# First layer of batch 0 with split operands instead of two plain blocks, in a fused attention and two-MLP kernel

## The chip, the cores and the metric

One core of a Trainium2 chip. The metric is the device time of one launch in microseconds (us), median of several runs.

## The reference

Attention over 4 batches, 12 heads, 448 positions and 64 channels per head, followed by two feed-forward networks on all 4 x 448 = 1792 tokens (width 768):

```
q_n, k_n = rmsnorm(q, g_q), rmsnorm(k, g_k)
attn = softmax(q_n @ k_n.T / 8);  x = (attn @ v) as 1792 x 768
h = sigmoid(x @ w_gate) * (x @ w_val);  y = h @ w_out        # 768 -> 1536 -> 768
r = relu(y @ w_in2) ** 2;               out = r @ w_out2     # 768 -> 2048 -> 768
```

The weights come as 64-bit floats and are converted on the core. The results must keep float32 accuracy.

## The kernel before

**Order of the work.** A prologue computes the attention of batch 0, two heads (a pair) at a time, six pairs. A first sweep (`sweep(0)`) then runs both networks of batch 0 with the attention of batch 1 in its gaps, a second sweep those of batch 1 with the attention of batches 2 and 3, and a last part does both networks of batches 2 and 3 together.

**Weights.** A block is 128 x 768 weights. Each goes through four steps that `next_block` keeps a few blocks ahead of their use (`w_ahead`): `w_load` (the 64-bit block into one of three `raw64` buffers, on SP's queue), `w_conv` (L167 on ACT, L171 and L175 on DVE make float32 of it in one of three `wraw` buffers), `w_store` (the float32 block to memory for the later sweeps, by a DMA that POOL issues), and `w_split` (L193 on ACT casts it to a high part in the multiplier's faster format fp32r, L194 on DVE leaves the low part, both in one of four `wsp` buffers).

**Products.** The activations are split the same way: `x_hi` (L365, ACT) and `x_lo` (L371, DVE) for each pair of heads. `mm3` then makes a product of three fp32r matmuls, high by high, high by low, low by high (all through `mm`, L566). The first two blocks of the first sweep are made otherwise: with `NPLAIN = 2` they are converted straight into a part of the tile `area`, not split, and multiplied in plain float32 (L915, 6 matmuls a block, each two records in the trace) by the unsplit attention output `xplain`. Behind each of these two blocks three `x_hi` and three `x_lo` follow, which the later blocks need.

**The prologue's order.** It is a list written by hand: `at(key, step)`, sorted by key, four keys to a pair of heads (`t = 4 * hp + c` for chunk c of pair hp). For a chunk, `s_mm` makes scores (L291, PE), `s_max` their maxima (L297, DVE), `s_exp` the exponentials (L309, ACT), `c_mm` transposes them (L327, PE), `c_copy` copies the transposes out (L336 on ACT, L337 on DVE). For a pair, `pv_mm` multiplies by v (L345) and transposes the reciprocal sums (L350), then come `x_rec` (L356, ACT) and `x_sum` (L361, DVE). The next pairs' inputs are squared, scaled (`stat_hat`, L265, DVE, after a power on POOL, L261), transposed (`a_mm`, L571, PE) and copied (`a_copy`, L283 on DVE, L285 on ACT). Into this list come loads, conversions and splits of the first weight blocks. Matmul accumulators are four tiles `acc`; a tile is reused when it has been copied out. A scheduler in the framework turns the list into a fixed order for each engine, and each engine runs its own in order; the first sweep is also its to arrange, while PE's order from the second sweep on is the program's.

Of the kernel before, what the change touches and what calls it, by code (L numbers as in the profile page):

```python
# [17 lines left out]
def attention_moe_moe2_kernel(  # L18
# [19 lines left out]
    KD = DM // 128  # L38
# [33 lines left out]
    def acc_tile():  # L72
        return acc_p.tile([128, 512], F32, tag="acc", name="acc")

    def att_tile():
        return att_p.tile([128, 2, 512], F32, tag="att", name="att")
# [21 lines left out]
    NB = len(one_sweep)  # L98
    W4 = NB - K2
    K4 = K2 // 2  # L100
    NPLAIN = 2
    wt = [[dram_p.tile([128, 768], F32, tag=f"wt{t}{g}", name=f"wt{t}{g}") for g in range(K4 // 2)] for t in range(4)]
    w32 = [dram_p.tile([128, 768], F32, tag=f"w{i}", name=f"w{i}") for i in range(NB)]
    w1s = [dram_p.tile([128, 1536], F32, tag=f"ws{p}", name=f"ws{p}") for p in range(K1)]
# [49 lines left out]
    def w_conv():  # L154
# [5 lines left out]
        lo, hi = r[:, :, 0], r[:, :, 1]  # L160
        if i < NPLAIN:
            t = plain_w[0][:, 768 * i:768 * (i + 1)]
# [21 lines left out]
    def w_split():  # L184
        i = pos["split"]
        pos["split"] += 1
        if pos["store"] <= i < NB:
            w_store()
        t = wraw.pop(i)
        if i < NPLAIN:  # L190
            return
        sp = wsp_p.tile([128, 2, 768], F32R, tag="wsp", name="wsp")
        nc.scalar.copy(out=sp[:, 0], in_=t)  # L193
        nc.vector.tensor_tensor(out=sp[:, 1], in0=t, in1=sp[:, 0].bitcast(F32), op=ALU.subtract)  # L194
        wsp[i] = sp

    def w_ahead(i):
        while True:
            if pos["split"] <= min(i + 3, pos["conv"] - 1):
                w_split()  # L200
            elif pos["conv"] <= min(i + (3 if pos["conv"] < NPLAIN + 2 else 4), pos["load"] - 1, pos["split"] + 2):
                w_conv()
# [155 lines left out]
    def x_sum(st):  # L358
        r = st["r"]
        dst = xplain[0][:, st["hp"]] if st["b"] == 0 else r  # L360
        nc.vector.tensor_tensor(out=dst, in0=st["o"], in1=r, op=ALU.mult)  # L361
        st["o"] = dst

    def x_hi(st):
        hi = nc.scalar.copy(out=xtile[st["b"]][:, 0, st["hp"]], in_=st["o"])  # L365
        if st["b"] == 0:
            tc.keep_in_program_order(hi)

    def x_lo(st):
        x, hp = xtile[st["b"]], st["hp"]  # L370
        nc.vector.tensor_tensor(out=x[:, 1, hp], in0=st.pop("o"), in1=x[:, 0, hp].bitcast(F32), op=ALU.subtract)  # L371
# [154 lines left out]
    xtile, xplain, xwhole = {}, {}, {}  # L526
# [16 lines left out]
    def block():  # L543
        wb = next_block()
        flush()
        return wb

    def flush():
        for fn, args in mid:
            fn(*args)  # L550
        mid.clear()

    def half(s, kk):
        return s == 1 and kk in (1, 3)
# [20 lines left out]
    def mm3(o, wb, kk, xh, xl, start, stop):  # L575
        wh, wl = wb[:, 0, kk], wb[:, 1, kk]
        mm(out=o, lhsT=wh, rhs=xh, start=start, stop=False)
        mm(out=o, lhsT=wh, rhs=xl, start=False, stop=False)
        mm(out=o, lhsT=wl, rhs=xh, start=False, stop=stop)

    def tmp(name):
        return tmp_p.tile([128, 512], F32, tag="tmp", name=name)[:, :N]
# [318 lines left out]
    def sweep(s):  # L901
# [5 lines left out]
        for m in range(K1):  # L907
            for i in range(2):
                o = acc_tile()[:, :N]
                wb = block()  # L910
                for kk in range(KD):
                    if s == 0 and m == 0 and i == 0 and kk == KD - 1:
                        yield
                    if s == 0 and 2 * m + i < NPLAIN:
                        nc.tensor.matmul(  # L915
                            out=o, lhsT=wb[:, 0, kk], rhs=xplain[0][:, kk],
                            start=(kk == 0), stop=(kk == KD - 1))
                    else:
                        mm3(o, wb, kk, x[:, 0, kk], x[:, 1, kk], kk == 0, kk == KD - 1)
                    if half(s, kk):  # L920
                        yield
                        flush()
                if s == 0 and 2 * m + i < NPLAIN:
                    for hp in range(3 * (2 * m + i), min(KD, 3 * (2 * m + i) + 3)):
                        st = {"b": 0, "hp": hp, "o": xplain[0][:, hp]}
                        x_hi(st)
                        x_lo(st)
                if i == 0:
                    t = tmp("t")
                    e = tmp("e")  # L930
                    nc.scalar.activation(out=e, in_=o, func=AF.Relu, scale=-1.0)
                    nc.scalar.activation(out=t, in_=o, func=AF.Abs)
                    nc.scalar.activation(out=e, in_=e, func=AF.Exp, scale=-1.0)
                    nc.scalar.activation(out=t, in_=t, func=AF.Tanh, scale=0.5)
                else:
                    nc.vector.tensor_tensor(out=e, in0=o, in1=e, op=ALU.mult)
                    nc.vector.scalar_tensor_tensor(out=e, in0=t, scalar=1.0, in1=e, op0=ALU.add, op1=ALU.mult)
                    nc.scalar.copy(out=ht[:, 0, m], in_=e)
                    low.tensor_tensor(out=ht[:, 1, m], in0=e, in1=ht[:, 0, m].bitcast(F32), op=ALU.subtract)
                yield  # L940
        y = xbuf(s)
        for j2 in range(KD // 2):
            for i in range(2):
                o = acc_tile()[:, :N]
# [21 lines left out]
        for m2 in range(K2 // 2):  # L966
            for i in range(2):
                m = 2 * m2 + i
                o = acc_tile()[:, :N]
# [6 lines left out]
                t = tmp("rl")  # L976
# [20 lines left out]
        for hf in range(2):  # L997
            accs = [acc_tile() for _ in range(nt)]
            for kb in range(K2 // 2):
                wb = block()  # L1000
                for c, (rr, c0, row) in enumerate(chunks):
                    o = accs[c][:, :384]
# [17 lines left out]
    pairs = {}  # L1020
# [152 lines left out]
    def prologue():  # L1173
# [22 lines left out]
        def at(key, fn, *args):  # L1196
            plan.append((key, len(plan), fn, args, rush[0]))
# [9 lines left out]
        def acc4():  # L1207
            return acc_tile().rearrange("p (k c) -> p k c", k=NF + 1)

        for i in range(len(keys)):  # L1210
            t = 4 * i
# [26 lines left out]
        for hp in range(HP):  # L1238
            key = (0, hp)
            rush[0] = (30, 300, 0)[min(hp, 2)]  # L1240
            for c in range(QC):
                t = 4 * hp + c
                at(t, lambda key=key, c=c: s_mm(pairs[key], c, att_tile()))
                at(t, lambda key=key, c=c: s_max(pairs[key], c))
                at(t + 0.5, lambda key=key, c=c: s_exp(pairs[key], c))
                at(t + 1.75, lambda key=key, c=c: c_mm(pairs[key], c, acc4(), acc4()))
                at(t + 2.25, lambda key=key, c=c: c_copy(pairs[key], c, (act, dve)))
            at(t + 2.5, lambda key=key: s_rec(pairs[key]))
            at(t + 3, lambda key=key: pv_mm(pairs[key], acc_tile()[:, :S], acc_tile()[:, :S]))
            at(t + 3.75, lambda key=key: x_rec(pairs[key]))  # L1250
            at(t + 4.25, lambda key=key: x_sum(pairs[key]))
        rush[0] = 0
        for t in (6, 9, 12, 15, 18, 20, 22, 24, 25):
            at(t, w_load)
        for c, t in ((0, 14), (1, 15), (0, 18), (1, 19), (0, 20), (1, 20.6), (0, 22), (1, 22.6), (0, 24), (1, 24.6), (0, 26), (1, 26.6)):
            at(t, w_split if c else w_conv)
        plan.sort(key=lambda e: e[:2])
        n = 0
# [107 lines left out]
```

## Time and profile before

| what | us |
|---|---|
| median of 3 runs | 1252.28 (1250.48 to 1255.31) |
| the profiled execution | 1250.23 |
| its span, first to last instruction | 1248.5 |
| PE busy | 1229.1 (98%) |
| DVE busy | 949.5 (76%) |
| ACT busy | 791.8 (63%) |
| mean granted TensorE clock | 0.997 of full speed |

The span is 1.7 us short of the execution's time. PE is the matmul engine, PEld its weight loads, DVE the vector engine, ACT the scalar engine, POOL GpSimd, and SP the queue that starts most transfers. A busy share is that of the time in which an instruction of the engine was under way; matmuls overlap, so the spacing of their starts says more than their durations. The order of the stages in time: prologue up to about 94 us, first sweep to about 403 us.

### The profile page before, as it was taken

How to read it: one execution, taken by the hardware profiler on the slowest of the kernel's cores; microseconds unless marked ns; L12 is line 12 of the kernel's file. 1: busy time of each engine (PE TensorE's matmuls, PEld its weight loads, DVE VectorE, ACT ScalarE, POOL GpSimd, SP SyncE). 2: the span in 40 equal slices, each digit the busy share in tenths (PEclk: the TensorE clock that was granted, in tenths of full speed). 3: DMA queues.
4: the chain of work that ended last, by engine and by line, in shares of the span. 5: the costliest groups of instructions: out<-in, count | busy, mean ns of one | idle time of the engine just before them, and what ended most of it. 6: DMA issues, size and time to landing. Idle time of an engine off the chain costs nothing.

```text
span 1248.5 us, 19159 instructions
## 1 busy us (share of the span) xinstructions
PE 1229.1 (98%) x6611; PEld 1081.9 (87%) x6611; DVE 949.5 (76%) x1494; ACT 791.8 (63%) x1605; POOL 224.8 (18%) x236
## 2 busy tenths in 40 slices
PE   8999999999999999999999999999999999999998
PEld 6547878878889988999898899999999999999998
DVE  6877988778975878888888766878875326879872
ACT  5776888667765877876798755675664223335451
POOL 3312222211120122232222110011222001110000
PEclk9999999999999999999999999999999999999999
DMA  5555999888896666787777443467798435775443
GB/s 129 122 173 197 297 319 282 264 260 245 257 311 187 153 152 162 174 188 183 172 186 174 116 112 87 136 176 179 198 225 204 98 98 145 174 179 143 127 141 112
DMA packets 200545, 225.81 MB, mean 181 GB/s; under 512 B 83968, under 2 KB 178176, under 8 KB 200448
## 3 DMA queue, kind: packets, MB, share of 16 engines
q1 hardware_dynamic: 177024, 175.36, 48.8%
q0 software_dynamic: 21568, 48.77, 17.9%
q8 instruction: 52, 0.85, 0.3%
q10 hardware_dynamic: 1856, 0.46, 0.2%
q14 instruction: 45, 0.37, 0.1%
HBM read 185.99 MB, written 76.28 MB: 210 GB/s over the span
## 4 chain that ended last, share of the span: by engine, by line
PE 86%; ACT 4%; DVE 3%; DMA 3%; issue 2%; SPq 1%; ACTq 0%; DVEq 0%
PE acc L566 55%; PE att L566 18%; PE att L571 3%; PE att L291 3%; DMA raw<-in_moe_w_gate_dram 2%; PE acc L345 2%; PE att L345 2%; PE acc L571 1%; PE acc L327 1%; PE att L327 1%; DMA wraw<-w 1%; ACT wraw L167 1%; DVE wsp L194 1%; ACT p L309 1%; ACT wsp L193 0%
## 5 line engine op out<-in xcount | busy, mean ns | idle before, releaser
L566 PE MATMUL acc<-xy,wsp 128*128 128x448 f32 x1404 | 310.8, 372 | 1.1 <-ACT rl L978 0.6
L193 ACT CAST wsp<-wraw 128x768 fp32r<-128x768 f32 x248 | 207.3, 837 | 161.0 <-PE acc L566 74.5
L194 DVE TENSOR_TENSOR wsp<-wraw,wsp 128x768 fp32r<-128x768 f32 x248 | 237.3, 958 | 84.6 <-ACT wsp L193 82.3
L566 PEld LDWEIGHTS acc<-xy,wsp 128*128 128x128 f32 x1404 | 258.5, 188 | 30.5 <-issue 6.4
L566 PE MATMUL att<-parts,wsp 128*128 128x448 f32 x720 | 152.4, 365 | 0.0
L566 PEld LDWEIGHTS att<-parts,wsp 128*128 128x128 f32 x720 | 135.1, 188 | 10.8
L566 PE MATMUL acc<-parts,wsp 128*128 128x448 f32 x540 | 116.0, 365 | 0.0
L261 POOL TENSOR_TENSOR ms<-ms,mhalf 112x16 f32<-112x16 f32 (+1 forms) x25 | 76.8, 3073 | 189.5 <-DVE ms L260 189.5
L566 PE MATMUL acc<-wsp,rb 128*128 128x384 f32 x576 | 109.6, 340 | 0.0
L566 PEld LDWEIGHTS acc<-parts,wsp 128*128 128x128 f32 x540 | 101.3, 188 | 8.0
L566 PEld LDWEIGHTS acc<-wsp,rb 128*128 128x128 f32 x576 | 100.4, 189 | 2.4 <-issue 2.0
L566 PE MATMUL acc<-hb,wsp 128*128 128x448 f32 x432 | 95.2, 371 | 0.0
L566 PE MATMUL acc<-h,wsp 128*128 128x448 f32 x432 | 87.7, 365 | 0.0
L566 PEld LDWEIGHTS acc<-hb,wsp 128*128 128x128 f32 x432 | 79.3, 188 | 9.3 <-issue 2.7
L566 PEld LDWEIGHTS acc<-h,wsp 128*128 128x128 f32 x432 | 81.1, 188 | 6.4
L167 ACT ACTIVATE wraw<-raw 128x768 f32<-128x768 f32 x66 | 60.2, 916 | 32.3 <-DVE wsp L194 16.6
L182 POOL DMA_DIRECT2D w<-wraw x66 | 36.5, 553 | 220.4 <-DVE wraw L175 202.0
L458 ACT ACTIVATE p<-att,nm 112x448 f32<-112x448 f32 x96 | 60.1, 631 | 17.2 <-DVE nm L447 16.2
L309 ACT ACTIVATE p<-att,nm 112x448 f32<-112x448 f32 x88 | 55.3, 637 | 17.9 <-DVE nm L297 16.3
L566 PE MATMUL acc<-wsp,rp 128*128 128x384 f32 x360 | 64.0, 334 | 0.0
L175 DVE SCALAR_TENSOR_TENSOR wraw<-wraw,raw 128x768 int32<-128x768 int32 x66 | 62.9, 954 | 0.9
L566 PEld LDWEIGHTS acc<-wsp,rp 128*128 128x128 f32 x360 | 62.6, 188 | 0.0
(205 smaller groups left out, 1992.3 us busy)
## 6 DMA issues: line engine op xcount, KB each, us to landing
wraw<-w SPq DMA_DIRECT2D x80, 384.0 KB, 3.6
w<-wraw POOLq DMA_DIRECT2D x66, 384.0 KB, 6.3
raw<-in_moe_w_out_dram SPq DMA_DIRECT2D x28, 768.0 KB, 6.6
wraw<-w SPq DMA_DIRECT2D x92, 192.0 KB, 2.6
raw<-in_moe_w_in_dram SPq DMA_DIRECT2D x16, 768.0 KB, 6.0
raw<-in_moe_w_gate_dram SPq DMA_DIRECT2D x12, 768.0 KB, 6.7
raw<-in_moe_w_val_dram SPq DMA_DIRECT2D x12, 768.0 KB, 7.1
ws<-w POOLq DMA_DIRECT2D x48, 192.0 KB, 4.8
```

Source lines behind the costliest of these rows:

```text
L167: size = nc.scalar.activation(out=t, in_=hi.bitcast(F32), func=AF.Prelu, scale=2.0 ** -112, alpha=2.0 ** 32)
L175: nc.vector.scalar_tensor_tensor(out=ti, in0=ti, scalar=3, in1=hi, op0=ALU.logical_shift_left, op1=ALU.bitwise_or)
L182: nc.gpsimd.dma_start(out=w32[i], in_=wraw[i])
L193: nc.scalar.copy(out=sp[:, 0], in_=t)
L194: nc.vector.tensor_tensor(out=sp[:, 1], in0=t, in1=sp[:, 0].bitcast(F32), op=ALU.subtract)
L261: nc.gpsimd.tensor_tensor(out=ms, in0=ms, in1=mhalf[:QR, 0:ms.shape[1]], op=ALU.pow)
L291: nc.tensor.matmul(out=ps[:QR, e, :S], lhsT=kq[a, 1, c * QR:(c + 1) * QR], rhs=kq[a, 0], start=True, stop=True)
L309: nc.scalar.activation(out=p[:, e], in_=ps[:QR, e, :S], func=AF.Exp, bias=nm[:, e:e + 1], scale=st["rq"][:, c, e:e + 1] if "rq" in st else ...
L345: nc.tensor.matmul(out=o[e * D:(e + 1) * D], lhsT=v[:, kc, e], rhs=pt[:, (NF + 1) * e + kc if kc < NF else NF], start=(kc == 0), stop=(kc ...
L458: nc.scalar.activation(out=p[:, i * S:(i + 1) * S], in_=ps[:QR, i, :S], func=AF.Exp, bias=nm[:, i:i + 1], accum_out=su[:, c, e:e + 1])
L566: m = latest[0] = nc.tensor.matmul(**kw)
L571: m = nc.tensor.transpose(*a)
```

## The change

No block is plain any more (`NPLAIN = 0`), so the first two blocks are converted into `wraw` buffers, split, and multiplied by `mm3` like the others. The `x_hi` and `x_lo` of each pair of heads stand in the prologue's list behind its `x_sum`. The list has six conversions and six splits of weights as before, with some keys changed; before, the first two splits did nothing but start the store. The nine `w_load` entries stand in the list before and after.

```diff
-    NPLAIN = 2
+    NPLAIN = 0
...
-                if s == 0 and 2 * m + i < NPLAIN:
-                    for hp in range(3 * (2 * m + i), min(KD, 3 * (2 * m + i) + 3)):
-                        st = {"b": 0, "hp": hp, "o": xplain[0][:, hp]}
-                        x_hi(st)
-                        x_lo(st)
...
             at(t + 4.25, lambda key=key: x_sum(pairs[key]))
+            at(t + 4.4, lambda key=key: x_hi(pairs[key]))
+            at(t + 4.45, lambda key=key: x_lo(pairs[key]))
...
-        for c, t in ((0, 14), (1, 15), (0, 18), (1, 19), (0, 20), (1, 20.6), (0, 22), (1, 22.6), (0, 24), (1, 24.6), (0, 26), (1, 26.6)):
+        for c, t in ((0, 14), (1, 15), (0, 18), (1, 19), (0, 19), (1, 20), (0, 22), (1, 23), (0, 24), (1, 24.6), (0, 25.5), (1, 26)):
             at(t, w_split if c else w_conv)
```

DVE's order where the first block is converted, in the attention of the third and fourth pair (`raw` is the 64-bit block, `nm` the maxima, `xy_267` the split activations):

```order
 L171 TENSOR_SCALAR raw_555<-raw_555 128x768
 L260 TENSOR_SCALAR ms<-ms 112x16
-L175 SCALAR_TENSOR_TENSOR area<-area,raw_555 128x768
+L175 SCALAR_TENSOR_TENSOR wraw<-wraw,raw_555 128x768
+L194 TENSOR_TENSOR wsp<-wraw,wsp 128x768
 L361 TENSOR_TENSOR xplain<-acc,rs 128x448
 L297 TENSOR_REDUCE nm<-att 112x2
 L337 COPY area<-acc 128x3x112
-L297 TENSOR_REDUCE nm<-att 112x2
-L316 TENSOR_SCALAR su<-su 112x8
+L371 TENSOR_TENSOR xy_267<-xplain,xy_267 128x448
+L297 TENSOR_REDUCE nm<-att 112x2
```

The low part of the block (L194) now stands ahead of `x_sum` and of the chunk maxima, and the low part of the activations (L371) ahead of the next maxima.

PE's order from the last pair's score matmuls to the first sweep, before:

```order
L915 MATMUL acc<-xplain,area 128x448 x4
L327 MATMUL acc<-ident,p 128x112 x3
L915 MATMUL acc<-xplain,area 128x448
L327 MATMUL acc<-ident,p 128x112 x11
L345 MATMUL acc<-area,v_93 64x448
L350 MATMUL acc<-ident,sb 128x112 x4
L345 MATMUL acc<-area,v_93 64x448 x7
L915 MATMUL acc<-xplain,area 128x448 x5
L566 MATMUL acc<-xy_267,wsp 128x448 x9
L915 MATMUL acc<-xplain,area 128x448 x2
L566 MATMUL acc<-xy_267,wsp 128x448 x56
```

and with the change:

```order
L566 MATMUL acc<-xy_267,wsp 128x448 x12
L327 MATMUL acc<-ident,p 128x112 x5
L566 MATMUL acc<-xy_267,wsp 128x448
L327 MATMUL acc<-ident,p 128x112 x2
L566 MATMUL acc<-xy_267,wsp 128x448 x2
L327 MATMUL acc<-ident,p 128x112 x7
L345 MATMUL acc<-area,v_93 64x448
L350 MATMUL acc<-ident,sb 128x112 x4
L345 MATMUL acc<-area,v_93 64x448 x7
L566 MATMUL acc<-xy_267,wsp 128x448 x101
```

Ahead of the last pair's `pv_mm` (L345) stood 5 of the 12 plain matmuls and now stand 15 of the 36 that replace them. Further on, the first sweep's attention instructions stand at other places among the matmuls, up to some blocks apart; from the start of the second sweep every engine's order is the same again.

ACT's order ahead of the last pair's `pv_mm`, with the change:

```order
L309 ACTIVATE p,su<-att,nm 112x448 x2
L167 ACTIVATE wraw<-raw_955 128x768
L167 ACTIVATE wraw<-raw_1019 128x768
L336 COPY area<-acc 128x4x112 x2
L167 ACTIVATE wraw<-raw_1082 128x768
L356 COPY rs<-acc 128x448
L365 CAST xy_267<-xplain 128x448
L193 CAST wsp<-wraw 128x768
```

Before, the same two conversions stood between the last exponentials and the two copies, and one split (L193) and two more `x_hi` behind them. The last L193 shown is now that of the fifth block, which waits until PE has used up the first block's `wsp` buffer.

## Rows read from the trace of the kernel before

**Rows 1.** The page's busy times, and its chain of work by engine:

```profile
PE 1229.1 (98%) x6611; PEld 1081.9 (87%) x6611; DVE 949.5 (76%) x1494; ACT 791.8 (63%) x1605; POOL 224.8 (18%) x236
...
PE 86%; ACT 4%; DVE 3%; DMA 3%; issue 2%; SPq 1%; ACTq 0%; DVEq 0%
```

**Rows 2.** PE's waits over the span: us in total, times, longest us.

```profile
PE acc L327 <- ACT p L309: 2.3, 4, 0.8
PE acc L571 <- DVE qk L265: 1.8, 1, 1.8
...
PE att L327 <- ACT p L309: 1.3, 2, 0.8
...
PE acc L566 <- DVE wsp L194: 1.1, 2, 0.7
...
PE acc L327 <- DVE area L337: 0.8, 1, 0.8
```

**Rows 3.** Timeline of PE, prologue: start us, us, line, tiles, count [idle before].

```profile
53.60 3.23 PE L345 MATMUL acc<-pt,v 128*64 128x448 f32 x16
...
65.32 3.23 PE L345 MATMUL acc<-area,v 128*64 128x448 f32 x16
...
76.46 3.23 PE L345 MATMUL acc<-pt,v 128*64 128x448 f32 x16
...
89.01 0.96 PE L345 MATMUL acc<-area,v 128*64 128x448 f32 x2
...
93.59 4.03 PE L915 MATMUL acc<-xplain,area 128*128 128x448 f32 x10
```

**Rows 4.** Timeline of PE, first sweep.

```profile
100.43 11.85 PE L566 MATMUL acc<-xy,wsp 128*128 128x448 f32 x56
...
119.35 3.52 PE L566 MATMUL acc<-xy,wsp 128*128 128x448 f32 x16 [0.38 <-DVE wsp L194]
```

**Rows 5.** Busy by engine (PE, PEld, DVE, ACT, POOL), granted clock, DMA share, GB/s.

```profile
40.00:60.00 20.00, 20.00 (x121) 9.68 (x120) 17.16 (x30) 15.69 (x40) 7.54 (x5) 1.00 0.18 38
60.00:80.00 20.00, 19.04 (x117) 9.71 (x117) 16.00 (x27) 16.21 (x41) 3.10 (x6) 1.00 0.55 165
80.00:100.00 20.00, 19.23 (x84) 10.27 (x81) 14.76 (x23) 11.03 (x22) 2.79 (x5) 1.00 0.78 246
```

**Rows 6.** Groups by line and shape, 0 to 200 us: count, busy us, mean ns.

```profile
L194 DVE TENSOR_TENSOR wsp<-wraw,wsp 128x768 fp32r<-128x768 f32 x25 | 23.7, 951 | 3.6 <-ACT wsp L193 3.3
...
L193 ACT CAST wsp<-wraw 128x768 fp32r<-128x768 f32 x25 | 21.0, 846 | 0.6 <-DVE wraw L175 0.6
...
L915 PE MATMUL acc<-xplain,area 128*128 128x448 f32 x24 | 9.9, 548 | 0.0
...
L371 DVE TENSOR_TENSOR xy<-xplain,xy 128x448 fp32r<-128x448 f32 x6 | 3.5, 619 | 0.0
```

**Rows 7.** Timeline of DVE: first conversion, and keys of the sixth pair.

```profile
56.30 0.96 DVE L175 SCALAR_TENSOR_TENSOR area<-area,raw 128x768 int32<-128x768 int32 x1
...
64.30 0.61 DVE L283 COPY kq<-acc 128x448 f32<-128x448 f32 x1
```

**Rows 8.** Timeline of ACT, end of the prologue.

```profile
86.37 1.72 ACT L167 ACTIVATE wraw<-raw 128x768 f32<-128x768 f32 x2
88.00 0.93 ACT L336 COPY area<-acc 128x448 f32<-128x448 f32 x2
...
92.12 1.50 ACT L365 CAST xy<-xplain 128x448 fp32r<-128x448 f32 x3
```

**Rows 9.** Busy by engine and granted clock, around PE's longest wait for `stat_hat`.

```profile
450.00:460.00 10.00, 8.21 (x38) 7.16 (x37) 7.57 (x14) 7.02 (x17) 2.53 (x4) 0.83 0.96 195
460.00:470.00 10.00, 10.00 (x58) 9.18 (x57) 8.53 (x14) 8.48 (x20) 2.27 (x3) 1.00 0.91 193
```

**Rows 10.** Timelines of POOL and DVE, a power and a split at the same time.

```profile
447.08 2.93 POOL L261 TENSOR_TENSOR ms<-ms,mhalf 112x16 f32<-112x16 f32 x1 [13.59 <-DVE ms L260]
...
448.15 0.95 DVE L194 TENSOR_TENSOR wsp<-wraw,wsp 128x768 fp32r<-128x768 f32 x1
```

## The prediction

> **What bounds the kernel now.** I read the page first. PE is busy for 98% of the span, and the chain that ended last runs through PE for 86% of it [rows 1]. So the time is PE's work and PE's waits, and an edit counts only where it alters one of the two. PE's waits over the whole span come next: they are few, mostly under 1 us, and the ones that this change can touch are those of the transposes for exponentials (L327), of a transpose for a DVE copy, and of a matmul for a weight split [rows 2]. The third view is PE's timeline over the prologue: two pairs of heads begin their products with v 11.72 us apart (53.60 and 65.32), the next 11.14 (76.46), the last 12.55 (89.01), with ten records of plain matmuls in between [rows 3]. The fourth says what else is loaded there: from 40 to 80 us DVE is busy for 80 to 86% and ACT for 78 to 81%, while between 80 and 100 ACT falls to 55% [rows 5]. The reader is to see that the prologue is PE's too, but with DVE close behind it. From 100 us on PE's order is one long row of matmuls with one short wait at 119 [rows 4].
>
> **The change part by part.** Times below are against the profiled execution, 1250.23 us (span 1248.5 and 1.7 around it); it is 2.05 below the median of the runs shown, 1252.28.
>
> *Matmul work.* Twelve plain matmuls go, 24 records. Ten of them last 4.03 us, of which the last one's own length is 0.55 [rows 3, 6], so they follow each other by (4.03 - 0.55) / 9 = 0.387, and 24 take 9.3 us. They become 36 fp32r matmuls, which follow each other by 11.85 / 56 = 0.21 [rows 4], 7.6 us. PE gets back 1.7 us, all of it on the path. Bounds: with 0.35 (3.48 over all ten) and 0.40 (4.03 over ten) for a record it is 0.8 and 2.0.
>
> *The pairs of heads.* What PE saves is paid for on DVE and ACT, ahead of the last pair's product with v. DVE gets two more splits there (L194, 0.95 us) and five `x_lo` (L371, 0.62), 5.0 us together; ACT two more casts (L193, 0.85) and five `x_hi` (L365, 0.5), 4.2 us [rows 6, 8]. The sixth `x_lo` and two further splits lie behind that product, under matmuls, and cost nothing while three blocks (54 matmuls, 11 us) are ready. Nor does the store of the first blocks cost: it leaves from `wraw` in place of `area`, and the next conversion into that buffer comes some 20 us later. The nine loads are nine before and after, and move no queue that PE waits for. In DVE's order the added L194 and L371 stand ahead of chunk maxima; behind these wait ACT's exponentials, and behind those PE's transposes. I went through the changed order by hand from 53 us on, with the spacings of the trace. The first block's conversion ends at 57.2 as before [rows 7]. Its cast and low part follow, so the next maxima are 0.9 us later and, behind the `x_lo`, those after them 1.3. DVE's copy of the sixth pair's keys, which frees the accumulator of the fourth pair's product with v, starts at 65.6 in place of 64.30 [rows 7], so that product starts at 66.3 (before 65.32). The fifth pair's then starts at 78.1 (before 76.46), as the second and third block are both split in front of it. The last pair's starts at 89.3 (before 89.01 [rows 3]): there ACT is what PE waits for, with two conversions and two copies behind the last exponentials, in the order they had before [rows 8]. Two `x_lo` of the earlier pairs may cost another 0.1 each, so 89.5. By then PE has made 15 matmuls of the first layer in place of ten records, 3.15 against 3.9 us, so with no new wait it would have been there at 88.3. The pairs thus cost 1.2 us of new waits. Bounds: 1.5 gained, if the waits before these transposes (0.8 on DVE's copy, 0.7 of the 2.3 on exponentials [rows 2]) vanish and no new one comes; 5.0 lost, if all that DVE gets falls on PE. I take 1.2, nearer the first, since DVE has 2.3 us spare in each 11.7 [rows 5].
>
> *The weights behind.* Block 7's split was late by 0.38 us at 119 [rows 4]. Now the first `wsp` buffer comes free at about 99.7, when the first block's last matmul is through, and the conversions behind it on ACT and DVE run some 5 us earlier than before; I expect the split about 2.7 us ahead of its use. That is 0.4 back. Bounds: 0 and 0.4.
>
> *The rest of the first sweep.* Its attention instructions stand at other places, with the same work. Two of the waits on exponentials, 1.3 us in all, lie here [rows 2], and may go or come again. I take 0, with 1.3 gained as one end and a wait like the 1.8 us one before `stat_hat` as the other [rows 2]. That one cost more than itself: around it PE began 38 matmuls in 10 us, where the next 10 us hold 58, so it took 20 / 58 of 10 us, 3.4 us, 1.6 of them because the granted clock was 0.83 on the mean, that is a third of the time at 1.2 GHz and not 2.4 [rows 9]. From the second sweep on nothing is moved.
>
> Sum: -1.7 + 1.2 - 0.4 = **-0.9 us**, 1249.3 for a profiled execution and 1251.4 for the median.
>
> **A rule against it.** A split that ran inside a power on POOL took 0.95 us, its mean, and the power 2.93, so neither held up the other [rows 6, 10]. The Trainium skill (SBUF — State Buffer, Who interferes with whom) says that a DVE instruction with two SBUF inputs and a GpSimd instruction that reads SBUF lock each other out, the one that issues second for all of the other's time. By that rule the added split would wait for the whole power; the trace does not agree.
>
> **The rivals.**
> - *DVE becomes the bound of the pairs.* The added 5.0 us fall on PE in full, and waits of more than a microsecond bring the lower clock as at 452 us, 1.6 more [rows 9]: -2.1 + 5.0 + 1.6 = +4.5, 1256.8. With `x_hi` (2.5 us) in series it would be 1259.3. For it: DVE's 86% [rows 5], and that maxima stand behind the added work. Against: DVE's spare time. It decides once the last product with v starts after 90.4 (88.3 and the 2.1 saved): from there the kernel is slower than before. Chance 0.20.
> - *All waits go.* -1.7 - 0.4 - 1.5 - 1.3 = -4.9, 1247.4. For it: the new order has more blocks ready early, and matmuls of the first layer fill PE between transposes. Against: the same exponentials must still come. Chance 0.15.
> - *The first sweep's new order makes one long wait*, as at 452: -0.9 + 3.4 = +2.5, 1254.8. For it: several hundred instructions change places, and DVE is then at over 80%. Against: there the trace has 0.38 and two waits under 1 us. Chance 0.15.
> - *DVE held off by POOL.* The added split of the first block falls into the power that POOL starts beside the conversion, and DVE stands still for up to that power's 2.93 us: -0.9 + 2.9 = +2.0, 1254.3. Chance 0.03, as the row speaks against it [rows 10].
>
> **How the numbers follow.** The forecast has the 0.47 that is left. About 0.5% of the time, 6.3 us, is what a measurement of this kernel can tell from no change. None of the gains adds up to that: 4.9 is all there is, so faster has 0.04, for the scatter of the medians. Slower needs DVE's work in series with ACT's: 0.08. The same has 0.88. The range goes from all waits gone, 1247.4, to DVE's work in full, 1256.8, with the outermost tenths left out: 1247.2 to 1256.4.
>
> **What would show it.** Right: L915 is gone, the last product with v starts between 88.5 and 90.4, the wait of block 7 is gone, and the first layer's matmuls follow each other by 0.21 from there on. The profile of the changed kernel would show DVE at 85% or more between 60 and 90 us. Wrong: that product starts after 90.4, or PE's waits between 100 and 400 us add up to more than 3 us, or the granted clock falls there. If block 7 still waits, the reasoning on the buffers is wrong, too.

## The result, and the profile after

The kernel after takes 1257.35 us (median of 9 runs, from 1254.57 up), the one before 1250.48 (9 runs, 1247.27 to 1256.22). One run of the kernel after, 6749.57 us, was disturbed, and the comparison leaves it out (the median of the other eight is 1256.67). The ratio is **1.0054**, with a 95% interval of 1.0039 to 1.0068: the change makes the kernel slower by 0.54%, 6.8 us (4.9 to 8.5 by the interval). The profiled execution took 1258.77 us. From its page, the span, the busy times and the chain, as in [rows 1]:

```profile
span 1257.0 us, 19177 instructions
...
PE 1233.2 (98%) x6623; PEld 1083.8 (86%) x6623; DVE 951.2 (76%) x1496; ACT 794.7 (63%) x1607; POOL 226.1 (18%) x236
...
PE 83%; DVE 5%; ACT 5%; DMA 3%; issue 2%; SPq 2%; POOL 0%; DVEq 0%; ACTq 0%; POOLq 0%
```

PE, DVE and ACT do nearly the work that they did. What has grown is the part of the chain that runs through DVE and ACT, from 7% to 10%: PE waits more for them. These shares only say where to look: three points are 38 us of the span, many times the loss. PE's timeline over the pairs of heads, to set beside [rows 3]:

```profile
56.00 3.23 PE L345 MATMUL acc<-pt,v 128*64 128x448 f32 x16
...
64.15 1.22 PE L327 MATMUL acc<-ident,p 112*128 112x112 f32 x7 [0.86 <-ACT p L309]
...
69.03 3.23 PE L345 MATMUL acc<-area,v 128*64 128x448 f32 x16
...
77.01 1.01 PE L291 MATMUL att<-kq 64*112 64x448 f32 x4 [0.85 <-ACT p L309]
...
79.29 1.22 PE L327 MATMUL acc<-ident,p 112*128 112x112 f32 x7 [0.44 <-ACT p L309]
...
81.37 0.97 PE L345 MATMUL acc<-pt,v 128*64 128x448 f32 x2
...
93.53 0.96 PE L345 MATMUL acc<-area,v 128*64 128x448 f32 x2 [1.10 <-ACT area L336]
...
98.10 20.74 PE L566 MATMUL acc<-xy,wsp 128*128 128x448 f32 x101
```

From the third product with v to the last it is 93.53 - 56.00 = 37.53 us, where it was 89.01 - 53.60 = 35.41. That is 2.1 us more, behind three waits on exponentials and one on a copy by ACT, 3.25 us together; before there were two, of 0.74 and 0.77. The first layer then runs 101 matmuls without a wait, and block 7's of [rows 4] is gone. The same stretches as in [rows 5], busy by engine and granted clock:

```profile
60.00:80.00 20.00, 17.55 (x109) 9.03 (x106) 18.03 (x30) 17.05 (x41) 5.71 (x6) 1.00 0.54 159
80.00:100.00 20.00, 18.89 (x97) 10.70 (x98) 15.19 (x25) 12.14 (x26) 2.77 (x5) 1.00 0.59 181
```

From 60 to 80 us, where this execution runs 2.4 us behind the one before, DVE went from 80% to 90% and ACT from 81% to 85%, and PE from 95% to 88%.

The second loss stands where the first sweep ends. PE's timeline there, of the kernel before:

```profile
373.15 2.55 PE L566 MATMUL acc<-wsp,rb 128*128 128x384 f32 x13
375.54 0.84 PE L327 MATMUL att<-ident,p 112*128 112x112 f32 x7
376.14 1.30 PE L566 MATMUL acc<-wsp,rb 128*128 128x384 f32 x6
377.28 0.93 PE L571 MATMUL att<-ident,qk 112*128 112x112 f32 x8
378.05 0.83 PE L327 MATMUL att<-ident,p 112*128 112x112 f32 x7
378.65 6.49 PE L566 MATMUL acc<-wsp,rb 128*128 128x384 f32 x36
```

and of the kernel after, with the second sweep's first product as the last line (403.25 before):

```profile
379.64 0.44 PE L566 MATMUL acc<-wsp,rb 128*128 128x384 f32 x1
379.92 0.84 PE L327 MATMUL att<-ident,p 112*128 112x112 f32 x7
381.72 0.98 PE L571 MATMUL att<-ident,qk 112*128 112x112 f32 x8 [0.96 <-ACT pt L337]
382.97 0.89 PE L327 MATMUL att<-ident,p 112*128 112x112 f32 x7 [0.26 <-ACT p L309]
385.58 6.86 PE L566 MATMUL acc<-wsp,rb 128*128 128x384 f32 x38 [1.72 <-ACT ob L1010]
...
410.20 0.98 PE L566 MATMUL acc<-xy,wsp 128*128 128x448 f32 x4
```

Before, 13 and 6 matmuls stood between the last groups of transposes; now 1 and none. ACT and DVE have no time to empty what the transposes fill, and PE waits 0.96 + 0.26 + 1.72 = 2.9 us. The scheduler has put the attention's last steps one block (18 matmuls) later, and the output copy (`ob`) on ACT behind four copies of keys and queries, which end at 385.0:

```profile
385.05 1.25 ACT L1010 COPY ob<-acc 128x384 f32<-128x384 f32 x3
```

No line of the diff touches this place.

From the last product with v to the second sweep the kernel after needs 410.20 - 93.53 = 316.67 us, the one before 314.24. Called **pairs** and **rest** from here on, the two stretches lose 2.1 + 2.4 = 4.5 us. The two profiled spans lie 8.5 apart. Of the other 4.0, 2.4 come before the third product with v (56.00 against 53.60) and 1.6 behind the start of the second sweep, where both orders are the same; the last section returns to both. So of the 6.8 us of the ratio the profiles place 4.5 in the two stretches.

### The profile page after: what moved, and what is told of

Read it like the earlier page. It is cut to its first block, busy times and chain, and to the rows that moved or that the text cites. A ratio compares the mean times of both kernels' runs of the same rounds, so it can differ in the third digit from the quotient of the medians.

```text
span 1257.0 us, 19177 instructions
## 1 busy us (share of the span) xinstructions
PE 1233.2 (98%) x6623; PEld 1083.8 (86%) x6623; DVE 951.2 (76%) x1496; ACT 794.7 (63%) x1607; POOL 226.1 (18%) x236
## 4 chain that ended last, share of the span: by engine, by line
PE 83%; DVE 5%; ACT 5%; DMA 3%; issue 2%; SPq 2%; POOL 0%; DVEq 0%; ACTq 0%; POOLq 0%
PE acc L566 56%; PE att L566 18%; PE att L571 3%; PE att L345 2%; PE att L291 1%; PE att L327 1%; DMA qk<-in_k_dram 1%; DVE nm L297 1%; PE acc L571 1%; ACT p L309 1%; ACT wsp L193 1%; PE acc L345 1%; DMA raw<-in_moe_w_val_dram 1%; SPq L236 1%; DVE wsp L194 1%
## 5 line engine op out<-in xcount | busy, mean ns | idle before, releaser
L566 PE MATMUL acc<-xy,wsp 128*128 128x448 f32 x1440 | 317.3, 371 | 1.2 <-ACT rl L973 1.0
L193 ACT CAST wsp<-wraw 128x768 fp32r<-128x768 f32 x250 | 209.0, 836 | 166.9 <-PE acc L566 82.5
L194 DVE TENSOR_TENSOR wsp<-wraw,wsp 128x768 fp32r<-128x768 f32 x250 | 240.2, 962 | 96.1 <-ACT wsp L193 94.3
L566 PEld LDWEIGHTS acc<-xy,wsp 128*128 128x128 f32 x1440 | 264.6, 188 | 33.1 <-issue 6.0
```

The lines of the kernel that those rows point to most:

```text
L566: m = latest[0] = nc.tensor.matmul(**kw)
```

## The experiments

Each was compared with runs of the kernel before on the same chip. All stretches are read from PE's timeline of one profiled execution each: pairs and rest as above, and the sum of the waits that the timeline shows between 100 and 400 us. keys_only was measured and profiled twice: its pairs differ by 0.02 us between the two executions, its rest by 0.65 and its waits by 0.5. Differences of that size in the rest are not read as effects.

| kernel | pairs | rest | waits | ratio to before, interval |
|---|---|---|---|---|
| before | 35.41 | 314.24 | 1.7 | 1 |
| after | 37.53 | 316.67 | 3.7 | 1.0054 [1.0039, 1.0068] |
| x_only | 35.55 | 318.74 | 5.1 | 1.0035 [1.0016, 1.0054] |
| keys_only | 35.41 | 313.95 | 1.2 | 0.9989 [0.9979, 0.9998] |
| keys_only_again | 35.43 | 314.60 | 1.7 | 0.9992 [0.9981, 1.0004] |
| split_pinned | 37.12 | 316.89 | 3.8 | 1.0049 [1.0032, 1.0065] |
| xlo_pool | 37.10 | 317.49 | 4.2 | 1.0034 [1.0020, 1.0049] |
| x_late | 38.40 | 316.20 | 3.3 | 1.0049 [1.0034, 1.0064] |
| splits_last | 35.90 | 325.69 | 8.7 | 1.0082 [1.0059, 1.0105] |
| splits_spread | 35.60 | 319.09 | 4.5 | 1.0049 [1.0032, 1.0066] |
| after_p64 | 37.50 | 323.49 | 7.3 | 1.0093 [1.0074, 1.0112] |
| before_p64 | 35.41 | 319.87 | 4.8 | 1.0032 [1.0019, 1.0045] |
| late_pace | 37.54 | 317.17 | 4.1 | 1.0058 [1.0035, 1.0080] |
| spread_late | 35.60 | 320.27 | 5.3 | 1.0069 [1.0045, 1.0092] |
| x_only_order | 35.55 | 315.16 | 2.1 | 0.9999 [0.9987, 1.0011] |
| after_order | 37.51 | 313.53 | 0.9 | 1.0010 [0.9998, 1.0021] |
| spread_order | 35.62 | 313.85 | 1.2 | 1.0008 [0.9998, 1.0019] |

### One part of the change at a time

**x_only**: the kernel after with

```
-    NPLAIN = 0
+    NPLAIN = 2
-        for c, t in ((0, 14), (1, 15), (0, 18), (1, 19), (0, 19), (1, 20), ...
+        for c, t in ((0, 14), (1, 15), (0, 18), (1, 19), (0, 20), (1, 20.6), ...
```

> Blocks 0 and 1 stay plain, with the order of conversions and splits of before; of the change only the split of x within the prologue is left (x_hi and x_lo behind every pair's x_sum). Two stretches of the PE timeline are compared: the pairs, from the third PV product to the last (53.60 to 89.01 before, 35.4 us; 56.00 to 93.53 after, 37.5 us), and the rest of the first sweep, from there to the second sweep's first product (314.2 us before, 316.7 after). Theory A (the splits of blocks 0 and 1, which were nothing before, stand in order ahead of x_sum and cost the pairs 2.1 us): pairs 35.4 to 36.0. Theory B (the split of x costs them): pairs 37 to 38. Theory C (the scheduler's new order near 380 us, with the output copy behind the key and query copies on ACT, costs 2.9 us of waits): this kernel has the new order, so the waits of PE between 370 and 390 come to 2.5 to 3.2 us. Ratio to before: A with C 1.002, B with C 1.004.

**keys_only**: the kernel before with

```
-        for c, t in ((0, 14), (1, 15), (0, 18), (1, 19), (0, 20), (1, 20.6), ...
+        for c, t in ((0, 14), (1, 15), (0, 18), (1, 19), (0, 19), (1, 20), ...
```

> The kernel before with the table of conversions and splits of the change; blocks 0 and 1 plain, x split in the sweep. Both A and B: pairs 35.2 to 35.9 us, since blocks 0 and 1 have no split and x none within the pairs. C: the order near 380 us is that of before, so no wait there, rest of the first sweep 313.5 to 314.8. Ratio 0.9990 to 1.0010. A rival D (the earlier conversions alone hold up the pairs): pairs over 36.5, ratio 1.0015 or more.

The split of x costs the pairs 0.14 us, so theory B is out. Yet x_only loses 4.4 us (0.0035 x 1249.4), with PE's timeline near the end of its first sweep:

```profile
378.45 0.98 PE L571 MATMUL att<-ident,qk 112*128 112x112 f32 x8 [0.96 <-ACT pt L337]
379.69 0.89 PE L327 MATMUL att<-ident,p 112*128 112x112 f32 x7 [0.26 <-ACT p L309]
382.30 6.89 PE L566 MATMUL acc<-wsp,rb 128*128 128x384 f32 x38 [1.72 <-ACT ob L1010]
```

These are the three waits of the kernel after, with plain blocks still there. Three more stand at 137 to 154 us, 1.74 together, and the ratio is above the 1.002 that A with C had. The earlier split of x alone brings a new order and these waits. The table of conversions alone brings neither: keys_only keeps the order of before and both stretches. Its ratio, just below 1, was measured once more:

> keys_only once more, in five rounds, for its ratio of 0.9989 [0.9979, 0.9998] is the only one below 1. If the earlier conversions alone are worth the 0.3 us that the rest of the first sweep was shorter by (313.95 against 314.24), the ratio lies at 0.9995 to 1.0000 and cannot be told from no change; if they are worth more, it comes out at 0.9985 to 0.9992 again.

It came out at 0.9992, with an interval of 0.9981 to 1.0004. That includes no difference, but it lies where the expectation put a gain of more than 0.3 us. Whether the table alone is worth some 0.1% stays open: the two profiles do not show it, with 313.95 and 314.60 us for the rest and 314.24 before.

### What the pairs wait for

DVE's timeline of the kernel after, where the first block is converted and split:

```profile
58.93 0.96 DVE L175 SCALAR_TENSOR_TENSOR wraw<-wraw,raw 128x768 int32<-128x768 int32 x1
60.78 0.96 DVE L194 TENSOR_TENSOR wsp<-wraw,wsp 128x768 fp32r<-128x768 f32 x1 [0.90 <-ACT wsp L193]
61.66 0.62 DVE L361 TENSOR_TENSOR xplain<-acc,rs 128x448 f32<-128x448 f32 x1
62.19 1.08 DVE L297 TENSOR_REDUCE nm<-att 112x2 f32<-112x896 f32 x1
```

and ACT's:

```profile
59.92 0.83 ACT L193 CAST wsp<-wraw 128x768 fp32r<-128x768 f32 x1
...
62.31 0.57 ACT L365 CAST xy<-xplain 128x448 fp32r<-128x448 f32 x1 [0.51 <-DVE xplain L361]
63.37 0.63 ACT L309 ACTIVATE p<-att,nm 112x448 f32<-112x448 f32 x1 [0.49 <-DVE nm L297]
```

The cast (L193) can't begin before DVE has the conversion done (59.9), and the low part (L194) can't begin before the cast is. So DVE, the fuller engine, stands still for 0.90 us and then works 0.96 on the low part, with `x_sum` and the maxima in line behind it. The exponentials that follow at 63.37 are those for which PE waits at 64.15. Block 1's split has the same idle time of 0.90 us, at 73.10.

**split_pinned**: both splits issued behind `x_lo` of their pair (keys 15.5 and 19.5) and held there.

```
-        for c, t in ((0, 14), (1, 15), (0, 18), (1, 19), (0, 19), (1, 20), (0, 22), ...
+        for c, t in ((0, 14), (1, 15.5), (0, 18), (0, 19), (1, 19.5), (1, 20.6), (0, 22), ...
+        if i < 2:
+            tc.keep_in_program_order(top)
+        if i < 2:
+            tc.keep_in_program_order(rest)
```

> The kernel after, but the splits of blocks 0 and 1 are issued behind x_hi and x_lo of their pair and held there on ACT and on DVE, so that no x_sum stands behind them. A: pairs 35.5 to 36.3 us instead of 37.5, the two idle times of DVE of 0.90 us ahead of the split of weights gone. B: pairs 37 to 38. C: rest of the first sweep as after, 316 to 317.5, with 2.5 to 3.2 us of waits near 380. Ratio to before: A 1.0035 to 1.0045, B 1.005 or more.

**xlo_pool**: `x_lo` on GpSimd within the prologue.

```
-            at(t + 4.45, lambda key=key: x_lo(pairs[key]))
+            at(t + 4.45, lambda key=key: x_lo(pairs[key], nc.gpsimd))
```

> The kernel after with x_lo on GpSimd within the prologue; DVE has 0.62 us less for each pair, the splits of blocks 0 and 1 stay where the change puts them. A: pairs still 36.8 to 37.8 us, the idle times of DVE of 0.90 us stay. B (DVE's added work): pairs 35.4 to 36.3. Rest of the first sweep as after. Ratio to before: A 1.0045 to 1.006, B 1.003 to 1.004.

**x_late**:

```
-            at(t + 4.4, lambda key=key: x_hi(pairs[key]))
+            at(23.45 if hp < HP - 1 else t + 4.4, lambda key=key: x_hi(pairs[key]))
```

and `x_lo` likewise.

> The kernel after, with x_hi and x_lo of the first five pairs issued together just ahead of block 0's first products, so that the pairs carry the splits of blocks 0 and 1 but no split of x up to there. If these splits of weights alone cost the pairs their 2.1 us: pairs 36.8 to 37.6. If it takes both (x alone cost 0.14 us in x_only): pairs 35.4 to 36.2. Rest of the first sweep as after, with the waits near 380. Ratio to before 1.0045 to 1.006 or 1.003 to 1.0045.

None of the three settled it. split_pinned missed the pairs that A had for it and came out in the range of B, which x_only had ruled out. The idle times of DVE ahead of the low parts went, and the fourth product with v came 0.6 us sooner (12.40 us behind the third, 13.03 after), about half of what it had lost. Yet the pairs got only 0.4 back: in the fifth, where the third conversion stands as well, DVE stands still for 1.42 us ahead of `x_sum`, ACT casts two blocks ahead of exponentials (at 74.12 and 75.69), and PE waits 1.40 us for these. So the idle times are a part of the loss and not the whole. xlo_pool gives 0.4 too; its pairs are those of A, its ratio that of B. x_late came out beyond both of its forecasts, but it shows the splits alone from the third product with v to the fifth: 24.58 us against 22.86 before, 23.00 with x alone (x_only) and 25.37 with both. So most of it, 1.7 of 2.5, is the two splits' own, and the splits of x that it delays cost more at the end: its last interval is 13.82 us where after had 12.16.

**splits_last**: both splits behind the last pair's first scores, the third conversion where the change has it. **splits_spread**: block 0's behind `x_lo` of its pair, block 1's and the third block's behind the last pair's first scores, the third conversion one step later. In splits_last the first two splits are held in the program's order as in split_pinned, in splits_spread all six.

```
-        for c, t in ((0, 14), (1, 15), (0, 18), (1, 19), (0, 19), (1, 20), (0, 22), (1, 23), ...
+        for c, t in ((0, 14), (0, 18), (0, 19), (1, 21), (1, 22), (0, 22.5), (1, 23), ...
```

and

```
-        for c, t in ((0, 14), (1, 15), (0, 18), (1, 19), (0, 19), (1, 20), (0, 22), (1, 23), ...
+        for c, t in ((0, 14), (1, 15.5), (0, 18), (0, 20), (1, 21), (1, 22), (0, 22.4), (1, 23), ...
```

> The kernel after, with the splits of blocks 0 and 1 issued behind the last pair's first scores (keys 21 and 22, held there on ACT and DVE) and the fifth and sixth split behind them; the split of x stays in the pairs. If the place of these two splits in the crowded fourth and fifth pair costs the 2.1 us: pairs 35.5 to 36.2. If any two more splits of weights before the last PV product cost it: pairs 36.8 to 37.6. Rest of the first sweep as after. Ratio to before 1.003 to 1.0045, or 1.005 and more.

> The kernel after with block 0's split behind x_lo of its pair, block 1's and the later ones behind the last pair's first scores, third conversion one step later, all six held there on ACT and DVE. Its PE order from the first layer's first products to the second sweep is that of after but for one matmul, so that only the pairs differ. Place of the splits as the cause of the pairs' loss: pairs 35.5 to 36.4 us, rest of the first sweep 316.3 to 317.5 with the 2.9 us near 380; ratio to before 1.0035 to 1.0045. If a later split makes the last PV product wait instead: last interval over 13.0 (12.2 after), pairs 37 or more, ratio 1.005.

PE's timeline of splits_spread, the same stretch:

```profile
53.82 3.23 PE L349 MATMUL acc<-pt,v 128*64 128x448 f32 x16
...
76.20 1.22 PE L331 MATMUL acc<-ident,p 112*128 112x112 f32 x7 [0.73 <-ACT p L313]
...
89.42 0.97 PE L349 MATMUL acc<-area,v 128*64 128x448 f32 x2 [1.14 <-ACT area L340]
```

89.42 - 53.82 = 35.60: with the same work at another place, and the same 15 matmuls of the first layer ahead of that product, the pairs take what they took before, but for 0.2 us. DVE is even fuller there: from 60 to 90 us it is busy for 92%, in the kernel after for 88%. So it is the place of the splits and of the third conversion, in the two fullest pairs, that cost 2.1 us, and not DVE's share. splits_last, which leaves that conversion where it was, gets 1.6 of it back. The rest is 2.4 us longer than after's, by 0.8 us of further waits and by slower matmuls behind them (last section). It was expected as in after, so the ratio missed its range, too, and shows nothing of the gain. splits_last needs 35.90 for the pairs, as expected, but the scheduler's order for it brings two new waits in the first sweep, of 1.92 us at 187.72 and 3.46 at 224.50.

### What the first sweep waits for

**after_p64** and **before_p64**, the kernels after and before with

```
-            want = min(total, i + 1 if s == 1 else (i + 1) * total // 66)
+            want = min(total, i + 1 if s == 1 else (i + 1) * total // 64)
```

> The kernel after with one number changed: the attention's steps are handed out over 64 instead of 66 steps of the first sweep, so that the scheduler puts 15 and 19 matmuls between the last three groups of transposes instead of 1 and 0. C (the back-to-back transposes near 380 us cost 2.9 us of waits and, in some executions, a fall of the clock behind them): PE waits under 0.5 us between 360 and 400, rest of the first sweep 313.5 to 315 instead of 316.7, pairs as after (37.3 to 37.7), ratio to before 1.0015 to 1.003. Rival (the waits only move to another place of the sweep): rest of the first sweep stays over 316, ratio 1.0045 or more.

> Control: the kernel before with the same number, 64. It had no wait near 380 us, so C expects nothing to gain: rest of the first sweep 313.5 to 315, pairs 35.4, ratio 0.999 to 1.001. If the pacing is worth something by itself wherever it stands, the ratio is below 0.9985 and after_p64 shows the same gain for that reason and not for C.

**late_pace**, and **spread_late** with 44 for 40 and the splits of splits_spread:

```
-            want = min(total, i + 1 if s == 1 else (i + 1) * total // 66)
+            want = min(total, i + 1 if s == 1 else (i + 1 + 2 * (i >= 40)) * total // 66)
```

> The kernel after with the attention's steps handed out two steps earlier from step 40 of the first sweep on (i + 3 in place of i + 1); up to about 320 us its order on PE is that of after. The scheduler then puts 13, 15 and 1 matmuls between the last groups of transposes, where after has 1, 0 and 0. C: the 2.9 us of waits at 381 to 386 go and none of their size comes before them: PE waits 100 to 360 under 1.5 and 360 to 400 under 0.5, rest of the first sweep 313.3 to 314.5 instead of 316.7; ratio to before 1.002 to 1.0035. Rival (every new order of the sweep costs some microseconds somewhere, as with 64 steps): rest of the first sweep 316 or more, a wait of over 2 us between 320 and 360; ratio 1.005 or more.

> Both repairs together: the splits as in splits_spread, the attention's steps two earlier from step 44 on. If the pairs and the end of the first sweep are the whole loss: pairs 35.5 to 36.4, rest of the first sweep 313 to 314.5, second sweep's start 402 to 404 (403.25 before), ratio to before 0.998 to 1.001. If the sweep's new order finds another wait: ratio 1.002 or more, with the wait in the rest of the first sweep.

All four went wrong, in the same way. In the three made from the changed kernel the waits near 380 us went, as meant (spread_late has another there, of 1.12 us at 384.94), and others came. after_p64:

```profile
184.84 5.47 PE L566 MATMUL acc<-xy,wsp 128*128 128x448 f32 x18 [2.89 <-ACT t L927]
...
318.19 5.15 PE L345 MATMUL att<-pt,v 128*64 128x448 f32 x16 [2.81 <-ACT pt L336]
```

and late_pace, which has after's order up to about 310 us:

```profile
310.91 0.89 PE L327 MATMUL att<-ident,p 112*128 112x112 f32 x7 [1.51 <-ACT p L309]
313.29 3.56 PE L345 MATMUL att<-pt,v 128*64 128x448 f32 x16 [1.49 <-ACT pt L336]
```

The control, before_p64, is slower than before by 0.32%, with one wait of 3.04 us at 312.19. So the order of before is a good one among those seen here, and an edit that makes the scheduler draw a new one may lose some microseconds at a place that the edit does not touch.

That leaves the question whether PE's order is the cause, or the work that now comes earlier on ACT and DVE. The 1450 PE instructions that both kernels issue from the third block on stand in the same order in the program; only the scheduler permutes them. **after_order**, **x_only_order** and **spread_order** are after, x_only and splits_spread with these held in the permutation of before:

```
+            want = [pe[n] for a, z in ORDER for n in range(a, min(z, len(pe)))]
+            for one_, two_ in zip(want, want[1:]):
+                tc.add_manual_dep(
+                    two_, one_.name,
+                    mybir.DependencyInfo(mybir.DependencyClass.NoSync, mybir.DependencyReason.SCHED_ONLY), reason="order")
```

> The kernel after with the 1450 PE instructions of the first sweep that both kernels share (from the third block's first product on) held in the order that they have before; ACT and DVE stay with the scheduler. If the scheduler's new order of PE makes the first sweep's loss: PE waits 100 to 400 as before, 1 to 2 us, rest of the first sweep 312 to 313 us (314.2 before less the 1.7 of matmul work and the 0.4 of block 7's wait that the change saves), pairs 37.5 as after, so that the two cancel: ratio to before 0.999 to 1.0015. If it is the earlier work on ACT and DVE and not PE's order: rest 315 or more, ratio 1.003 or more.

> x_only (plain blocks, x split within the prologue) in the held order: the split of x costs the pairs 0.14 us as in x_only, and with PE's order of before the rest of the first sweep is 313.8 to 314.5 instead of 318.7; ratio 0.999 to 1.001 instead of 1.0035. If the loss of x_only has another cause, the rest stays over 317.

> The splits of splits_spread and the held order of after_order together. If the place of the splits and PE's order are the whole loss: pairs 35.5 to 35.8, rest of the first sweep 312 to 313, second sweep's start at most 401.5; ratio to before 0.9975 to 0.9995, the change's saving of 1.7 to 2.1 us come through. If not, ratio 1.001 or more and the wait that shows where.

PE's timeline of after_order, at the place of the three waits:

```profile
376.96 2.55 PE L568 MATMUL acc<-wsp,rb 128*128 128x384 f32 x13
379.35 0.84 PE L329 MATMUL att<-ident,p 112*128 112x112 f32 x7
379.95 1.30 PE L568 MATMUL acc<-wsp,rb 128*128 128x384 f32 x6
381.09 0.93 PE L573 MATMUL att<-ident,qk 112*128 112x112 f32 x8
381.86 0.83 PE L329 MATMUL att<-ident,p 112*128 112x112 f32 x7
382.46 6.50 PE L568 MATMUL acc<-wsp,rb 128*128 128x384 f32 x36
```

No wait is left. x_only goes from 1.0035 to 0.9999, and after from 1.0054 to 1.0010, while its pairs stay at 37.51. That shows the order as the cause: 0.36 and 0.44 points, 4.5 and 5.5 us, hang on the permutation, and the earlier work on ACT and DVE costs the first sweep nothing that can be told. From the intervals of the ratios I estimate that each of the two is uncertain by 2 to 3 us. Of the 5.5 us the profiled rest shows 316.67 - 313.53 = 3.1. What is held is PE's order; the scheduler then drew ACT's anew, too, and put the output copy back ahead of the keys and queries:

```profile
380.98 1.26 ACT L1012 COPY ob<-acc 128x384 f32<-128x384 f32 x3
```

The rests of both lie above their forecasts, after_order's by 0.5 us (313.53, where at most 313 was expected), x_only_order's by 0.7 (315.16 and 314.5).

spread_order missed its forecast. The pairs are as expected for the repairs (35.62), but the rest is 0.9 us above its range (313.85), and the change's own saving does not come through: the two together are 349.47 us, and 349.65 before. The ratio, 1.0008, is no difference that can be told, and its interval leaves at most 0.02% for a gain. Not all of the pairs' loss is gone in it: the fourth product with v still comes 12.40 us behind the third, where it was 11.72. With the two side effects repaired so far, the change is worth nothing that this measurement can see, and no kernel with the change in it beats the one before.

## Why the prediction was wrong

**The rest of the first sweep: "I take 0".** This is the step that failed. It is worth +3.1 us in the profile (after against after_order) and 5.5 by the ratios. The forecast had a price near it: its rival with one long wait stood at 3.4. In the profile it came otherwise, as three waits, all on ACT, with the granted clock at 1.00. It had the chance wrong, 0.15, on the ground that the trace of before has only 0.38 us and two short waits there. But that trace shows the one order that is given up, and says nothing on the one that comes. The eleven kernels here whose first sweep was drawn anew, wholly or from some point on, have 3.3 to 8.7 us of waits; the five in the order of before have 0.9 to 2.1. The eleven are not eleven separate draws, as seven of them share the three waits near 380 us, and that a new draw mostly loses is shown for this kernel alone.

**The pairs of heads: "1.2 us of new waits".** The mechanism was right, the size was not: counted as there, from 88.3 - 53.6 = 34.7 us without a new wait, they were 37.53 - 34.7 = 2.8. The forecast put the fourth, fifth and last product with v at 12.7, 24.5 and 35.7 to 35.9 us behind the third; they came at 13.03, 25.37 and 37.53. Two things were missed. The hand walk gave each split its own duration on DVE and left out that DVE stands still for 0.90 us ahead of it, until ACT's cast is through. It did not count `x_sum` either, though the order shown before the prediction has it behind L194. That makes up a part, as split_pinned shows. And the walk let the last pair make good 1.2 to 1.4 us of the delay, as PE waits for ACT there; it made good 0.4 (2.5 us late at the fifth product, 2.1 at the last). For ACT was late itself. The first of its last two exponentials, in the kernel before and after:

```profile
85.13 0.64 ACT L309 ACTIVATE p<-att,nm 112x448 f32<-112x448 f32 x1 [0.23 <-DVE nm L297]
```

```profile
89.67 0.63 ACT L309 ACTIVATE p<-att,nm 112x448 f32<-112x448 f32 x1 [2.07 <-DVE nm L297]
```

They start 31.53 and 33.67 us behind the third product, 2.14 later, and from them to the last product it is 3.88 and 3.86. So the whole loss of the pairs lies ahead of DVE's last maxima. DVE at 88% from 60 to 90 us was foreseen (at least 85%). The rival that DVE becomes the bound came half true: 2.8 us of new waits, of the 5.0 that it put at most. Of the 5.4 us between the forecast's -0.9 and the 4.5 of the two stretches, the pairs thus make up 1.6 and the order 3.1.

**Matmul work: -1.7.** L915 is gone, and 101 matmuls take 20.74 us, 0.205 each, as forecast. About 0.7 of the saving lies ahead of the last product with v, where PE waits for ACT anyway, and it vanishes there. Of the 1.0 behind it the rest in the held order has 0.7 and 0.4 us (313.53 and 313.85 against 314.24), which is not more than two executions of one kernel differ by: the saving is not shown.

**Block 7's split: -0.4.** Gone after, as forecast. In the held order it waits again, 0.36 us, so it was the order, too, and not the earlier buffers alone.

**DVE held off by POOL.** The first block's split did fall into a power on POOL, in the timeline of the kernel after:

```profile
59.05 3.59 POOL L261 TENSOR_TENSOR ms<-ms,mhalf 112x16 f32<-112x16 f32 x1 [4.39 <-DVE ms L260]
```

L194 ran from 60.78 for 0.96 us inside it, its usual duration; what it waited for was ACT. As in [rows 10], the trace does not agree with the rule of the Trainium skill (SBUF — State Buffer, Who interferes with whom). The power was not held up by the split either: in the kernel before it lasted as long, with no split in it.

```profile
56.42 3.60 POOL L261 TENSOR_TENSOR ms<-ms,mhalf 112x16 f32<-112x16 f32 x1 [4.39 <-DVE ms L260]
```

**The numbers.** What two of the rivals had foreseen came together, at part of the first one's price and nearly the whole of the second's in the profile, and the forecast had let each come alone. So the range ended at 1256.4, under the 1256.8 of a rival that had 0.20, and "slower" had 0.08. The signs named as "wrong" did appear: the last product with v came after 90.4 (93.53, or 91.1 without the 2.4 us that this execution had lost before the third), and the waits between 100 and 400 us add up to 3.7. The third, a fall of the granted clock there, did not in this profile: it is 1.00 from 100 to 400 us.

## What to carry to other kernels

Where a scheduler draws the order, an edit early in the program can cost some microseconds anywhere in the stretch that is drawn anew, as here in all eleven kernels that had a new draw; a trace of the old order can't rule that out, so the cost of a new draw belongs into the sum and not only among the rivals. To learn what an edit is worth by itself, hold the order of the instructions that both kernels share and compare again. A split that goes from DVE to ACT and back keeps DVE waiting for ACT's cast as well (0.90 us here, beside 0.96 for the low part) when nothing stands between; but look where the other work goes, too, for filling that gap gave back 0.4 of the 2.1 us, and another place for the splits and one conversion 1.9.

## What was not expected of the hardware

A wait can cost more than itself behind it. Seven kernels have the same three waits near 380 us, 2.9 us together. In after and x_only the 38 matmuls behind them take 6.86 and 6.89 us; in the other five, 37 or 38 of them take 8.28 to 8.45, some 1.6 more. In split_pinned, PE's timeline:

```profile
381.67 8.45 PE L570 MATMUL acc<-wsp,rb 128*128 128x384 f32 x38 [1.72 <-ACT ob L1014]
```

and the busy times by engine with the granted clock (0.83, third from the end):

```profile
380.00:390.00 10.00, 8.33 (x38) 8.13 (x38) 3.58 (x6) 4.81 (x9) 0.19 (x1) 0.83 0.61 157
```

The clock is 0.83 on the mean there, a third of the time at 1.2 GHz in place of 2.4, and in after and x_only it stays 1.00 from 380 to 390 us. So the profiled execution of the kernel after shows the loss at that place at its smaller size. That may be part of why the ratios give the order 5.5 us and the profile 3.1, and the difference of the two lies at the edge of what the ratios are uncertain by. How often the clock falls over many runs was not measured. The prediction's first rival has the clock fall behind waits of more than a microsecond; here a wait of 1.72 us left it at 1.00 in two executions and not in five.

The clock also fell in the first 30 us of three profiled executions, with no difference in the program up to there. The kernel after and before, 20 to 30 us:

```profile
20.00:30.00 10.00, 9.87 (x40) 5.50 (x41) 5.67 (x13) 6.62 (x17) 2.35 (x2) 0.56 0.61 149
```

```profile
20.00:30.00 10.00, 9.02 (x60) 5.32 (x60) 8.13 (x17) 8.14 (x21) 3.51 (x2) 1.00 0.62 145
```

In after, spread_late and after_order the third product with v starts at 56.0, in all others between 52.5 and 53.9, in after_p64 and late_pace, which have after's prologue, at 52.77 and 52.68. These 2.4 us belong to the execution, not to the change. Nor does the 1.6 behind the start of the second sweep: from there to the end of the span, with PE in the same order, it is 846.8 us after and 845.3 before, and between 841.3 and 847.0 over the profiles. What sets the clock in one execution and not in the next stays open.
